# One cycle per batch from batch 2 on, with batch 2 loaded by transposed DMAs

## The chip, the cores and the metric

The kernel runs on one core of a Trainium2 chip. The metric is the time of one execution on the device in microseconds (us), the median of several runs. The core's engines work in parallel, each through its own list of instructions in order: PE (TensorE, matrix products; PEld are its weight loads), ACT (ScalarE), DVE (VectorE), POOL (GpSimd, here mostly an issuer of DMAs that convert types) and SP (SyncE, here an issuer of DMAs). They meet through semaphores.

## The reference

Attention with 12 heads over 8 batches of 448 tokens, with one added to the denominator, and behind it two dense layers with a squared ReLU between them:

```python
q, k, v: (8, 12, 448, 64) float32
scores = q @ k.T / 8
m = max(scores)
e = exp(scores - m)
attn = e / (sum(e) + exp(-m) + 1e-9)
x = (attn @ v) as (3584 tokens, 768)
h = x @ w_in                    # 768 -> 2048
out = (max(h, 0) ** 2) @ w_out  # 2048 -> 768, float32
```

The maximum cancels out: e / (sum + exp(-m)) is exp(s) / (sum exp(s) + 1), and the kernel computes it without m.

## The kernel before, in words

Work is in float16 with sums in float32. A **quad** is four heads of a batch (three quads a batch), a **chunk** is 64 keys (seven a quad). `QUADS` numbers the quads from batch 1 on: m = 0 to 2 are batch 1, and so on. The kernel gives Tile a schedule by hand: strings of steps, which are issued in exactly the order in which they stand. A step's letter names a function, its numbers are arguments:

- `s` scores of a chunk (PE, L400; 4 or 8 instructions on quarters of the array), `e` their exp (ACT, L432, one instruction of 128 x 896)
- `a` one of four adds that reduce a quad's seven exps (DVE, L435), `S` the sum over keys by a product with ones (PE, L451), `Z` Ln of sum + 1 and `M` exp of its negative, so the reciprocal (ACT, L460 and L465)
- `v` one chunk of exps times values (PE, L470), `X` values times reciprocal into `xt` (two DVE instructions, L482); `xt`'s six blocks of 128 rows come in pairs, a pair from each quad
- `j` two of the six products of a first-layer tile (128 of the 2048 columns, L513; a tile is `j n,0,2`, `j n,2,4`, `j n,4,6`, and each pair needs one quad's `X`), `k` ReLU (ACT or DVE, L521), `l` square into `gs` (DVE, L524)
- `o` some of the 16 products of an output tile (128 tokens by 384 columns, L554; each in four quarter-array instructions into two PSUM banks), `O` the first half of the result to SBUF (ACT if its last number is 1, otherwise DVE; L571), `Q` the second half added and the store issued on SP (L579)
- `T` and `U` transposes of a quad's q or k on PE and the copy to SBUF (L203, L210); `i`, `r`, `g` the first layer of half of batch 0 (L530, L500, L507); `p`, `b`, `y`, `z`, `n`, `x` the same attention steps for halves of batch 0 (L312 to L383)
- `d n` issues the n-th entry of `LOADS` (L626), or in a cycle one of `following` (L716)

**How q and k come in.** Batches in `ON_PE` (0, 1, 2) are loaded naturally by GpSimd in quads and transposed on PE. Later batches go through DRAM: `stage` (L144) copies q and k as float16 to a DRAM tensor (GpSimd), `transposed_load` (L163) reads three planes of it with a transposing DMA on SP, and `tail_keys` (L178) has GpSimd gather the last 64 keys of each head. `load_v_quads` brings v.

**Stages.** `ORDER` (L676) covers all of the attention of batches 0 to 3, the first layer of batches 0 and 1 and 14 output tiles. Then comes `CYCLE` (L750), run twice, for b = 4 and 6: first layer of batches b-2 and b-1 (32 tiles), attention of batches b and b+1, 14 output tiles. The tail (L793) is the first layer of batches 6 and 7 and the 15 output tiles that are left, plainly in a loop. In `ORDER` and in the tail a first-layer product takes all 128 columns of a tile (L496), in `CYCLE` two instructions of 64 columns (`cols`, L494). Tail output tiles use whole-array products (L567).

**Buffers that set who waits for whom.** PSUM: two score tiles (`sp`, also used by `S`), and from step `P0` on a ring of four banks: a `j` tile takes one (free after `k`), an `o` tile two (free after `O` and `Q`), a quad's `v` two (free after `X`). SBUF: two `rt` for ReLU, two `half` for the adds, two `rcp`, four output tiles `ot` (free when their store has landed), two `qk`, two `vn`. `gs` is a ring of two batches.

Of the kernel before, what the change touches and what calls it, by code (L numbers as in the profile page):

```python
# [16 lines left out]
def kernel(  # L17
# [654 lines left out]
    def other_ring():  # L672
# [8 lines left out]
        z2 b1,2 p6 s15 b1,3 p7 e15 y1 b3,0 n2 x2 b3,1 z1 s17 e17 b3,2 p12 p13 b3,3 n1 s18 p14 s16 e18 p15 x1 y3 T1,1,0 U1,1,0,0,7,0 e16 b4,0 z3 b4,1
        s19 e19 i0,6 n3 r0,6,0 s20 e20 s21 i0,7 s22 x3 b4,2 e21 p16 b4,3 e22 b5,0 r0,7,0 p17 p18 p19 d4 b5,1 g0,6 y4 z4 n4 s23 T1,1,1 e23 d13 s27 b5,2
        x4 i0,4 s28 p20 p21 g0,7 b5,3 e27 p22 p23 y5 U1,1,1,0,7,0 e28 z5 r0,4,0 n5 x5 s26 s29 e26 j20,0,2 j23,0,2 j23,2,4 j20,2,4 j20,4,6 e29 j23,4,6
        s25 k23,1 s24 g0,4 e25 e24 k20,0 P0 i1,7 j19,0,2 l23 a0,0 s32 e32 a0,1 s36 d6 j19,2,4 e36 j16,0,2 l20 j19,4,6 j17,0,2 s34 s33 k19,1 r1,7,0
        j17,2,4 j16,2,4 a0,2 l19 e34 j17,4,6 e33 j16,4,6 g1,7 s30 d11 k16,1 s31 e30 k17,0 T2,0,0 T1,2,0 T2,0,1 T1,2,1 l16 s35 e31 U2,0,0,0,7,0
        U1,2,0,0,7,0 s37 U2,0,1,0,7,1 e35 j18,0,2 j18,2,4 e37 j18,4,6 a0,3 i1,6 d19 S0 U1,2,1,0,7,0 v0,0 a1,0 v0,1 Z0 v0,2 l17 v0,3 v0,4 v0,5 k18,0 d7
        d12 v0,6 s40 s43 M0 r1,6,0 j27,0,2 a1,1 e43 j22,0,2 j22,2,4 j27,2,4 X0 e40 j27,4,6 l18 j22,4,6 g1,6 a1,2 s39 k27,1 s38 e39 a1,3 d20 T2,2,0 e38
        k22,0 T2,2,1 T2,1,1 T2,1,0 s41 U2,2,1,0,7,1 U2,2,0,0,7,0 s42 j26,0,2 l27 e41 j21,0,2 j26,2,4 j26,4,6 l22 S1 U2,1,0,0,7,0 e42 U2,1,1,0,7,0 Z1
        v1,0 v1,1 v1,2 v1,3 v1,4 d23 v1,5 k26,1 v1,6 a2,0 a2,1 a2,2 s44 s47 M1 l26 e44 j21,2,4 d22 j21,4,6 i1,4 X1 a2,3 k21,1 v2,0 v2,1 v2,2 r1,4,0 S2
        e47 v2,3 Z2 v2,4 v2,5 l21 v2,6 M2 o0,0,4 s46 o0,4,8 d14 s50 e46 e50 o0,8,12 X2 o0,12,16 s51 g1,4 s48 O0,1 Q0 j15,0,2 j0,0,2 j15,2,4 j4,0,2  # L690
        j15,4,6 j4,2,4 j4,4,6 j0,2,4 e51 e48 j0,4,6 s45 k15,1 l15 o2,0,4 s49 e45 e49 o2,4,8 s52 d21 o2,8,12 a3,0 e52 o2,12,16 k4,1 k0,0 s53 a3,1 s55
        d24 j10,0,2 O2,1 j1,0,2 Q2 j10,2,4 j1,2,4 j10,4,6 l0 j14,0,2 l4 j1,4,6 j11,0,2 e55 k10,0 j14,2,4 a3,2 j11,2,4 k1,1 j8,0,2 l10 j14,4,6 j11,4,6
        k11,1 j9,0,2 a3,3 j8,2,4 j9,2,4 e53 l1 j8,4,6 j9,4,6 k14,0 s57 l14 e57 l11 S3 Z3 v3,0 d25 v3,1 v3,2 v3,3 k9,0 k8,0 v3,4 v3,5 v3,6 M3 o1,0,4
        s54 o1,4,8 X3 s56 o1,8,12 o1,12,16 e54 a4,0 O1,0 s63 e56 o5,0,4 s58 o5,4,8 Q1 e63 a4,1 a4,2 s65 e58 a4,3 o5,8,12 e65 s60 o5,12,16 e60 O5,1 s59
        v4,0 v4,1 Q5 v4,2 v4,3 l9 S4 v4,4 e59 Z4 M4 v4,5 v4,6 o4,0,4 o4,4,8 s61 o4,8,12 o4,12,16 e61 s64 O4,1 X4 s62 j2,0,2 l8 Q4 j2,2,4 j2,4,6 j7,0,2
        k2,1 j5,0,2 e62 j7,2,4 j7,4,6 k7,0 l7 d27 j12,0,2 j6,0,2 e64 a5,0 j12,2,4 j5,2,4 l2 j5,4,6 k5,1 j6,2,4 j6,4,6 j12,4,6 a5,1 j13,0,2 j13,2,4
        j13,4,6 l5 a5,2 j3,0,2 j3,2,4 j3,4,6 k12,0 a5,3 s69 l12 k6,1 o3,0,4 l6 k13,1 k3,1 l3 S5 l13 o3,4,8 o3,8,12 o3,12,16 O3,0 Q3 e69 s70 Z5 s71 d26
        M5 v5,0 v5,1 v5,2 v5,3 e70 e71 v5,4 v5,5 v5,6 o9,0,2 o9,2,4 X5 o9,4,6 o9,6,8 s66 o9,8,10 s68 o9,10,12 o9,12,14 o9,14,16 e66 O9,0 o6,0,2 e68
        s67 s72 o6,2,4 o6,4,6 o6,6,8 e67 o6,8,10 Q9 a6,0 a6,1 e72 a6,2 s73 o8,0,2 o6,10,12 o6,12,14 o8,2,4 o6,14,16 s75 e73 O6,0 o8,4,6 o8,6,8 e75 s78
        Q6 o8,8,10 o8,10,12 a6,3 e78 o8,12,14 s79 o8,14,16 s77 v6,0 v6,1 v6,2 v6,3 e79 e77 v6,4 S6 v6,5 v6,6 Z6 M6 s74 O8,0 Q8 o7,0,2 o7,2,4 e74 X6  # L700
        o7,4,6 s76 e76 a7,0 o7,6,8 o7,8,10 o7,10,12 o7,12,14 a7,1 o7,14,16 s82 d28 o10,0,2 O7,1 o10,2,4 o10,4,6 Q7 o10,6,8 s80 a7,2 e82 o10,8,10
        o10,10,12 o10,12,14 o10,14,16 e80 s85 s83 o11,0,2 o11,2,4 e85 o11,4,6 o11,6,8 d31 O10,1 Q10 e83 s81 a7,3 d29 o11,8,10 o11,10,12 o11,12,14 e81
        o11,14,16 O11,1 Q11 s84 o12,0,2 s86 o12,2,4 o12,4,6 e84 e86 o12,6,8 o12,8,10 a8,0 o12,10,12 o12,12,14 o12,14,16 S7 a8,1 O12,0 o13,0,4 o13,4,8
        d30 o13,8,12 Z7 Q12 a8,2 o13,12,16 v7,0 v7,1 v7,2 v7,3 O13,1 v7,4 a8,3 v7,5 v7,6 M7 S8 Q13 v8,0 v8,1 Z8 v8,2 v8,3 M8 v8,4 v8,5 X7 v8,6 X8
# [7 lines left out]
    def period(b):  # L712
        m = NQ * (b - 1)
        first = EARLY + 2 * KC * (b - FIRST_PERIOD) // 2

        def following(n):  # L716
            ahead, what = ((1, n) if n < 6 else (2, 6) if n < 7 else (1, 6) if n < 8 else (2, n - 8))
            t = b + ahead
            if t < B and (n != 7 or b > FIRST_PERIOD):
                if what < 3:  # L720
                    transposed_load(t, what)
                elif what < 5:
                    tail_keys(t, (what - 2,))
                elif what == 5:
                    load_v_quads(t)
# [100 lines left out]
```

## Time and profile before

| | us |
|---|---|
| runs: median (lowest to highest of 3) | 392.35 (391.83 to 393.56) |
| the profiled execution, by the same clock as the runs | 393.06 |
| its span, first to last instruction | 391.3 |
| opening, to the first first-layer product of the first cycle | 0 to 135.7 |
| first cycle (b = 4): first layer / attention and output tiles | 135.7 to 172.1 / to 225.8 |
| second cycle (b = 6): first layer / attention and output tiles | 225.8 to 262.2 / to 315.5 |
| tail | 315.5 to 391.3 |

The page cuts the span into 40 slices of 9.8 us; a digit is the busy share in tenths (9 is 90% or more):

```profile
PE   9789999999999999999999999999999999999997
DVE  2887995765666766556968757566778788880000
ACT  5999998586689511349988731248988730001221
DMA  8999999999939899903129596941112200001132
```

ACT is full in the opening and in the attention parts of the cycles and nearly idle in their first-layer parts. The DMA engines are full for the first 100 us, in which all the weights and the first batches come in.

### The profile page before, as it was taken

What the parts mean: (1) busy time and instruction counts of PE and PEld (TensorE: products, weight loads), DVE (VectorE), ACT (ScalarE), POOL (GpSimd) and SP (SyncE); (2) the same over time, 40 slices, a digit from 0 to 9 for tenths busy, and PEclk for the clock granted to TensorE, in tenths of its full rate; (3) what the DMA queues carried; (4) which work ended last, traced back from release to release, by engine and by line L of the source; (5) the groups of instructions that cost most, each with busy time, mean ns of one, the idle gap of its engine ahead of it and who ended that gap; (6) DMA issues with size and microseconds to landing.
All of it is one profiled execution on the core that took longest, in us unless ns stands there. A gap on an engine that the chain in (4) does not pass through costs nothing.

```text
span 391.3 us, 14259 instructions
## 1 busy us (share of the span) xinstructions
PE 383.2 (98%) x6432; PEld 253.7 (65%) x6432; DVE 251.9 (64%) x468; ACT 228.5 (58%) x308; POOL 62.2 (16%) x96
## 2 busy tenths in 40 slices
PE   9789999999999999999999999999999999999997
PEld 5566656565789755667777665667777755556665
DVE  2887995765666766556968757566778788880000
ACT  5999998586689511349988731248988730001221
POOL 8544420025000701300001240310000000000000
PEclk9999999999999999999999999999999999999999
DMA  8999999999939899903129596941112200001132
GB/s 143 203 205 205 202 203 205 182 182 175 215 75 175 158 195 149 160 2 66 44 54 194 145 182 131 151 46 44 52 55 64 64 23 2 0 0 61 62 82 80
DMA packets 75052, 45.34 MB, mean 116 GB/s; under 512 B 47472, under 2 KB 72944, under 8 KB 74992
## 3 DMA queue, kind: packets, MB, share of 16 engines
q0 software_dynamic: 24752, 22.62, 37.4%
q1 hardware_dynamic: 49952, 21.59, 28.1%
q8 instruction: 50, 0.82, 0.9%
q10 hardware_dynamic: 288, 0.23, 0.2%
q14 instruction: 10, 0.08, 0.1%
HBM read 45.69 MB, written 17.93 MB: 163 GB/s over the span
## 4 chain that ended last, share of the span: by engine, by line
PE 86%; ACT 6%; DMA 2%; SPq 2%; DVE 1%; issue 1%; POOL 1%; ACTq 0%; POOLq 0%; DVEq 0%
PE mp L93 77%; PE sp L93 8%; ACT et L254 4%; SPq L166 2%; DMA nn<-in_k_dram 2%; PE mp L207 1%; DMA out_dram<-ot 1%; ACT rcp L372 1%; ACT nn L254 0%; DVE qk L217 0%; ACT rcp L365 0%; ACT ot L575 0%; DVE half L341 0%; ACT rcp L463 0%; DVE half L447 0%
## 5 line engine op out<-in xcount | busy, mean ns | idle before, releaser
L93 PE MATMUL mp<-wout,gs 64*64 64x384 f16 (+2 forms) x2928 | 165.2, 322 | 0.0
L93 PE MATMUL mp<-xt,win 128*64 128x448 f16 (+2 forms) x1188 | 148.3, 347 | 0.1
L93 PEld LDWEIGHTS <-gs 64*64 64x64 f16 (+1 forms) x2928 | 103.1, 106 | 34.5
L93 PEld LDWEIGHTS <-win 128*64 128x64 f16 (+1 forms) x1188 | 83.2, 106 | 63.5 <-issue 4.2
L254 ACT ACTIVATE et<-sp 128x896 f16<-128x896 f32 (+2 forms) x131 | 110.6, 889 | 12.3 <-PE sp L93 11.7
L505 DVE TENSOR_SCALAR rt<-mp 128x448 f16<-128x448 f32 x87 | 54.1, 622 | 17.4 <-PE mp L93 14.5
L509 DVE TENSOR_TENSOR gs<-rt 128x448 f16<-128x448 f16 x128 | 47.8, 390 | 22.1 <-ACT rt L503 20.2
L503 ACT ACTIVATE rt<-mp 128x448 f16<-128x448 f32 x41 | 21.8, 543 | 65.0 <-PE mp L93 55.7
L575 ACT ACTIVATE ot<-mp 128x384 f32<-128x384 f32 (+2 forms) x31 | 14.9, 480 | 71.6 <-PE mp L93 68.8
L93 PE MATMUL sp<-qk 64*64 64x224 f16 (+1 forms) x1056 | 53.7, 274 | 2.1 <-DVE qk L217 0.5
L93 PEld LDWEIGHTS <-qk 64*64 64x64 f16 x1056 | 32.7, 115 | 15.2 <-issue 6.5
L188 POOL COPY flatq<-qk 64x384 f16<-64x384 f16 x20 | 14.8, 739 | 172.7 <-DMA qk<-stage_k 126.0
L254 ACT ACTIVATE nn<-sp 128x896 f16<-128x896 f32 x42 | 37.1, 916 | 4.3 <-PE sp L93 4.2
L487 DVE TENSOR_TENSOR xt<-mp,rcp 128x448 f16<-128x448 f32 x42 | 24.2, 619 | 15.7 <-ACT rcp L466 10.3
L581 DVE SCALAR_TENSOR_TENSOR ot<-mp,ot 128x384 f32<-128x384 f32 x42 | 23.4, 556 | 15.3 <-ACT ot L575 12.4
...
L93 PE MATMUL mp<-et,vn 64*64 64x448 f16 (+1 forms) x448 | 24.5, 343 | 0.0
L577 DVE TENSOR_SCALAR ot<-mp 128x384 f32<-128x384 f32 x26 | 14.4, 555 | 14.3 <-PE mp L93 14.2
L463 ACT ACTIVATE rcp<-sp,one_b 128x896 f32<-128x896 f32 x21 | 21.1, 1007 | 2.8 <-PE sp L93 2.7
L466 ACT ACTIVATE rcp<-rcp 128x896 f32<-128x896 f32 x21 | 19.9, 949 | 0.5
L441 DVE TENSOR_TENSOR half<-et 128x1792 f16<-128x1792 f16 x15 | 16.3, 1088 | 4.3 <-ACT et L254 4.2
L443 DVE TENSOR_TENSOR half<-half,et 128x1792 f16<-128x1792 f16 x15 | 16.3, 1086 | 0.3
...
## 6 DMA issues: line engine op xcount, KB each, us to landing
...
```

The source lines that it names most:

```text
L93: return nc.tensor.matmul(out_, lhsT, rhs, start=start, stop=stop)
L254: nc.scalar.activation(out=out_, in_=in_, func=AF.Exp, scale=scale)
L441: nc.vector.tensor_add(esq[m], a[:, 0:w], a[:, w:2 * w])
L443: nc.vector.tensor_add(esq[m], esq[m], z[:, 0:w])
L463: nc.scalar.activation(out=rcp, in_=zp[:, :, 0:S], func=AF.Ln, bias=one_b)
L466: nc.scalar.activation(out=zqs[m], in_=zqs[m], func=AF.Exp, scale=-1.0)
L487: nc.vector.tensor_mul(xts[b][:, 2 * g + i, :], xqs[m][i][:, 0:S], zqs[m][:, i, :])
L503: nc.scalar.activation(out=rt[:, 0:m], in_=hp[:, 0:m], func=AF.Relu)
L505: nc.vector.tensor_scalar(out=rt[:, 0:m], in0=hp[:, 0:m], scalar1=0.0, scalar2=None, op0=ALU.max)
L509: nc.vector.tensor_mul(gs[:, f0:f0 + per, t0 % RING:t0 % RING + n], r, r)
L575: nc.scalar.activation(out=ot, in_=op[:, 0:w], func=AF.Copy, scale=OUT_SCALE)
L581: nc.vector.scalar_tensor_tensor(out=ot, in0=lo[:, 0:w], scalar=OUT_SCALE, in1=ot, op0=ALU.mult, op1=ALU.add)
```

## The change

`ON_PE` shrinks to batches 0 and 1. The opening now has all the attention of batches 0 and 1, the first layer of batch 0, and 6 output tiles. From batch 2 on there is one cycle per batch, run six times: first layer of batch b-1 in 64-column form (16 tiles), then attention of batch b with seven output tiles; loads are for batch b+1. The tail keeps the first layer of batch 7 and 9 output tiles (seven full, two narrow). The orders of the steps are new throughout.

```diff
-    ON_PE = (0, 1, 2)
+    ON_PE = (0, 1)
...
-    EARLY = 14
-    FIRST_PERIOD = 4
+    EARLY = 6
+    FIRST_CYCLE = 2
...
-    LOADS = ([lambda b=b, g=g: load_quad(b, g) for b in range(3) for g in range(NQ) if b + g]
+    LOADS = ([lambda b=b, g=g: load_quad(b, g) for b in range(2) for g in range(NQ) if b + g]
              + [lambda b=b, g=g: load_v_quads(b, g, g + 1) for b in range(2) for g in range(NQ)]
-             + [lambda: load_v_quads(2)]
              + [lambda i=i: load_win(i, NW) for i in range(NW)]
              + [lambda n0=n0, y=y: load_wout(n0, y, 2) for n0 in (0, HALF) for y in range(2)]
-             + [lambda: stage(3), lambda: transposed_loads(3), lambda: tail_keys(3), lambda: load_v_quads(3),
-                lambda: stage(4), lambda: transposed_loads(4), lambda: tail_keys(4), lambda: load_v_quads(4), lambda: stage(5)])
+             + [lambda: stage(2), lambda: load_v_quads(2)]
+             + [lambda i=i: transposed_load(2, i) for i in range(3)]
+             + [lambda i=i: tail_keys(2, (i,)) for i in (1, 2)])
...
     ORDER = """
...
+        n3 b4,1 r0,7,0 x3 s20 b4,2 e20 s21 i0,6 e21 b4,3 s22 p16 p17 d12 e22 p18 d11 p19 b5,0 y4 i0,4 r0,6,0 b5,1 z4 s23 n4 T1,1,1 e23 s27 b5,2 e27 x4
+        g0,7 b5,3 p20 d15 r0,4,0 p21 U1,1,1,0,7,0 p22 p23 g0,4 d4 y5 s29 z5 s28 g0,6 j7,0,2 n5 j7,2,4 j6,0,2 j6,2,4 x5 e28 j6,4,6 e29 j7,4,6 k6,0 l6
+        k7,1 P0 s25 s24 j10,0,2 j10,2,4 j10,4,6 d16 j0,0,2 j0,2,4 k10,0 d17 l7 j0,4,6 k0,0 l0 j11,0,2 j5,0,2 j11,2,4 l10 j5,2,4 j11,4,6 d8 k11,1
+        j3,0,2 j2,0,2 j5,4,6 j2,2,4 l11 e24 k5,1 j3,2,4 j4,0,2 j3,4,6 j1,0,2 e25 j4,2,4 j4,4,6 j2,4,6 k2,1 l5 k3,0 j1,2,4 l2 d18 d9 l3 k4,1 j1,4,6
+        k1,0 i1,6 l4 l1 i1,7 r1,7,1 T1,2,1 r1,6,0 T1,2,0 U1,2,0,0,7,0 s26 s30 e30 e26 a0,0 g1,7 o0,0,2 U1,2,1,0,7,1 o0,2,4 o0,4,6 o0,6,8 o0,8,10
+        o0,10,12 o0,12,14 g1,6 o0,14,16 a0,1 s37 s31 i1,4 O0,1 e37 r1,4,0 s32 g1,4 e31 o2,0,2 o2,2,4 s33 o2,4,6 a0,2 d19 o2,6,8 o2,8,10 e32 s34 e33 Q0
+        o2,10,12 d10 a0,3 o2,12,14 e34 o2,14,16 O2,0 Q2 s35 v0,0 v0,1 v0,2 e35 S0 v0,3 v0,4 v0,5 Z0 v0,6 M0 X0 s39 d22 o3,0,2 o3,2,4 s41 o3,4,6 e39
+        e41 o3,6,8 o3,8,10 o3,10,12 o1,0,2 o3,12,14 o3,14,16 s43 O3,0 Q3 e43 s36 o1,2,4 e36 o1,4,6 o1,6,8 o1,8,10 a1,0 o1,10,12 a1,1 o1,12,14 s42 a1,2
+        o1,14,16 O1,1 s38 a1,3 o5,0,2 Q1 e42 d23 o5,2,4 e38 o5,4,6 s40 e40 d25 o5,6,8 a2,0 S1 o5,8,10 o4,0,2 o5,10,12 o4,2,4 Z1 o5,12,14 o5,14,16 s44
+        d20 o4,4,6 o4,6,8 a2,1 M1 O5,1 o4,8,10 o4,10,12 o4,12,14 Q5 a2,2 v1,0 e44 a2,3 v1,1 o4,14,16 d24 O4,1 v1,2 v1,3 v1,4 v1,5 d21 Q4 S2 v2,0 v2,1
+        v2,2 v1,6 v2,3 Z2 v2,4 M2 v2,5 v2,6 X1 X2
     """
...
-    def period(b):
+    def cycle(b):
         m = NQ * (b - 1)
-        first = EARLY + 2 * KC * (b - FIRST_PERIOD) // 2
+        first = EARLY + KC * (b - FIRST_CYCLE)
...
         def following(n):
+            if b + 1 < B:
+                if n < 3:
+                    transposed_load(b + 1, n)
+                elif n < 5:
+                    tail_keys(b + 1, (n - 2,))
+                elif n == 5:
+                    load_v_quads(b + 1)
                 else:
-                    stage(t)
+                    stage(b + 1)
...
-            "j": lambda n, c0, c1: later_in(*block(n), c0, c1, True),
+            "j": lambda n, c0, c1: later_in(b - 1, n, c0, c1, True),
...
     CYCLE = """
+        j4,0,2 j4,2,4 j5,0,2 j5,2,4 j2,0,2 d5 j4,4,6 k4,1 j5,4,6 j2,2,4 l4 j6,0,2 j6,2,4 k5,0 j11,0,2 j6,4,6 j2,4,6 k2,0 l2 l5 k6,1 l6 j9,0,2 j9,2,4
...
+        k12,1 l13 j8,0,2 j8,2,4 d6 j10,2,4 d1 l12 k1,0 l1 j8,4,6 j10,4,6 k8,0 s0,5 o0,0,2 e0,5 s0,0 k10,0 l8 e0,0 o0,2,4 o0,4,6 o0,6,8 o1,0,2 s0,4
...
+        O6,1 s2,6 o4,8,10 e2,6 d3 o4,10,12 Q6 o4,12,14 d4 a2,2 o4,14,16 O4,1 a2,3 Q4 M1 v1,0 v1,1 v1,2 v1,3 v1,4 v1,5 S2 v1,6 v2,0 v2,1 v2,2 v2,3 v2,4
+        v2,5 X1 Z2 M2 v2,6 X2
     """
-    for b in range(FIRST_PERIOD, B, 2):
-        STEPS = period(b)
+    for b in range(FIRST_CYCLE, B):
+        STEPS = cycle(b)
...
-    for b in (B - 2, B - 1):
-        for f0 in range(NFFB):
-            tile_in(b, f0)
+    for f0 in range(NFFB):
+        tile_in(B - 1, f0)
```

In the new `LOADS` d0 to d4 are quads of batches 0 and 1, d5 to d10 their v, d11 to d14 quarters of `w_in`, d15 to d18 of `w_out`, d19 the stage of batch 2, d20 its v, d21 to d23 its three transposed loads (q, then the two planes of k), d24 and d25 its tail keys. In a cycle d0 to d2 are the transposed loads, d3 and d4 the tail keys, d5 v and d6 the stage of batch b+1.

More of the change, by code (lines that the diff above doesn't have):

```diff
@@ L525, in later_squared @@
         squared((b, "all", f0), S * b, S, f0, 1)
-    def of_tile(n):
-        return (1, n) if n < NFFB else (0, n - NFFB)
     def half_in(half, pair, c0, c1):
@@ L655 @@
         "y": lambda n: half_sum(n % NQ, n // NQ),
-        "j": lambda n, c0=0, c1=DCH: later_in(*of_tile(n), c0, c1),
-        "k": lambda n, act: later_relu(*of_tile(n), act),
-        "l": lambda n: later_squared(*of_tile(n)),
+        "j": lambda n, c0=0, c1=DCH: later_in(0, n, c0, c1),
+        "k": lambda n, act: later_relu(0, n, act),
+        "l": lambda n: later_squared(0, n),
         "d": lambda n: LOADS[n](),
@@ L681 @@
[L681 to L704, printed above, removed]
+        d0 W8 c0,0,1 d5 c1,0,1 c1,4,0 t0,0,0 t1,0,0 u0,0,0,0 t1,0,4 u1,0,0,0 c0,4,1 t0,0,4 u1,0,4,1 d1 s0 u0,0,4,1 t0,1,0 u0,1,0,0 t1,1,0 d2 e0 d7 s1
@@ new lines @@
+        u1,1,0,0 s2 t0,1,4 t1,1,4 e1 u1,1,4,1 u0,1,4,0 e2 s12 T0,1,0 T0,1,1 U0,1,0,0,4,0 U0,1,1,0,4,0 U0,1,1,4,7,0 s3 p0 b0,0 e12 s4 e3 p2 s6 p3 d6
+        U0,1,0,4,7,0 e4 s5 e6 b0,1 p1 b0,2 b0,3 e5 T0,2,0 y0 U0,2,0,0,4,0 T0,2,1 U0,2,1,0,4,0 U0,2,0,4,7,0 d14 U0,2,1,4,7,0 s9 z0 n0 b1,0 e9 x0 s11
+        T1,0,0 e11 s8 T1,0,1 e8 b1,1 s10 U1,0,1,0,7,0 e10 s13 b2,0 U1,0,0,0,7,0 b2,1 e13 b2,2 p8 s14 e14 b1,2 s7 p9 b2,3 e7 p4 s15 b1,3 p10 p11 y2 p5
+        p6 p7 y1 b3,0 e15 d3 z2 b3,1 s17 z1 s18 n2 x2 n1 b3,2 e17 p12 d13 p13 p14 p15 e18 s16 b3,3 e16 y3 x1 T1,1,0 s19 z3 U1,1,0,0,7,0 i0,7 e19 b4,0
@@ L708 @@
         STEPS[step[0]](*(int(y) for y in step[1:].split(",")))
-    def period(b):
+    def cycle(b):
         m = NQ * (b - 1)
-        first = EARLY + 2 * KC * (b - FIRST_PERIOD) // 2
+        first = EARLY + KC * (b - FIRST_CYCLE)
         def following(n):
[L717 to L725, printed above, removed]
-                else:
-                    stage(t)
-        def block(n):
-            return b - 2 + n // NFFB, n % NFFB
+            if b + 1 < B:
[5 more added lines that the diff above has]
+                    load_v_quads(b + 1)
+                else:
+                    stage(b + 1)
         return {
@@ L755 @@
-        l19 j18,0,2 j12,4,6 j18,2,4 j18,4,6 j9,0,2 k18,1 j9,2,4 j20,0,2 k12,1 l18 j20,2,4 j11,0,2 j9,4,6 l12 j20,4,6 d4 k9,0 j11,2,4 k20,1 l9 j5,0,2
-        j11,4,6 l20 k11,0 j29,0,2 j5,2,4 j5,4,6 k5,1 j29,2,4 l5 j29,4,6 l11 j1,0,2 j4,0,2 j1,2,4 k29,0 j25,0,2 j25,2,4 j1,4,6 j8,0,2 j4,2,4 j4,4,6
-        k1,1 j8,2,4 j2,0,2 j25,4,6 j2,2,4 l1 l29 j8,4,6 j2,4,6 k4,0 j28,0,2 k25,0 l25 l4 j28,2,4 j24,0,2 j28,4,6 e0,3 d5 k2,1 j24,2,4 k8,1 j23,0,2
-        j24,4,6 j10,0,2 j23,2,4 l8 j10,2,4 j10,4,6 l2 k24,0 j23,4,6 k10,1 s0,4 l24 k28,0 l10 k23,0 e0,4 s0,5 o0,0,2 o0,2,4 o0,4,6 o0,6,8 o0,8,10
@@ new lines @@
+        l11 k14,1 k0,0 l14 l0 j13,0,2 j1,0,2 j3,4,6 j1,2,4 j13,2,4 j15,4,6 j13,4,6 k15,1 k3,0 j12,0,2 j12,2,4 l15 j12,4,6 j10,0,2 j1,4,6 l3 k13,0
+        k12,1 l13 j8,0,2 j8,2,4 d6 j10,2,4 d1 l12 k1,0 l1 j8,4,6 j10,4,6 k8,0 s0,5 o0,0,2 e0,5 s0,0 k10,0 l8 e0,0 o0,2,4 o0,4,6 o0,6,8 o1,0,2 s0,4
+        o0,8,10 l10 s0,1 o0,10,12 o0,12,14 e0,4 e0,1 o0,14,16 s0,3 O0,1 Q0 o1,2,4 o1,4,6 e0,3 o1,6,8 s0,2 o1,8,10 o1,10,12 o2,0,2 o1,12,14 e0,2 s0,6
+        e0,6 o2,2,4 s1,6 o1,14,16 a0,0 o2,4,6 O1,0 o2,6,8 e1,6 s1,1 o2,8,10 o2,10,12 s1,2 e1,1 o2,12,14 o2,14,16 a0,1 s1,5 Q1 e1,2 o3,0,2 e1,5 O2,0
@@ new lines @@
+        o3,2,4 s1,4 e1,4 o3,4,6 a0,2 o3,6,8 o3,8,10 s1,3 a0,3 o3,10,12 o3,12,14 Q2 e1,3 s1,0 o3,14,16 O3,0 e1,0 Q3 v0,0 S0 v0,1 Z0 M0 v0,2 v0,3 v0,4
+        v0,5 v0,6 s2,0 e2,0 o5,0,2 d0 o5,2,4 o5,4,6 s2,4 o5,6,8 o5,8,10 e2,4 o5,10,12 s2,3 a1,0 X0 a1,1 a1,2 a1,3 d2 o5,12,14 o5,14,16 s2,1 e2,3
+        o6,0,2 o6,2,4 s2,2 e2,1 o6,4,6 O5,1 o6,6,8 o6,8,10 Q5 s2,5 o6,10,12 o6,12,14 o4,0,2 e2,2 S1 e2,5 o6,14,16 Z1 a2,0 a2,1 o4,2,4 o4,4,6 o4,6,8
+        O6,1 s2,6 o4,8,10 e2,6 d3 o4,10,12 Q6 o4,12,14 d4 a2,2 o4,14,16 O4,1 a2,3 Q4 M1 v1,0 v1,1 v1,2 v1,3 v1,4 v1,5 S2 v1,6 v2,0 v2,1 v2,2 v2,3 v2,4
```

31 lines of the change are left out of this document (5 added, 26 removed).

## The prediction

> **What bounds the kernel now.** First the engines' shares (busy us, share of the span, instructions), then the busy time of each engine by stage.
>
> ```profile
> PE 383.2 (98%) x6432; PEld 253.7 (65%) x6432; DVE 251.9 (64%) x468; ACT 228.5 (58%) x308; POOL 62.2 (16%) x96
> ```
>
> ```profile
> 0.00:33.40 33.40, 28.89 (x577) 20.05 (x578) 23.90 (x57) 28.80 (x46) 19.19 (x32) 1.00 1.14 187
> 33.40:135.70 102.30, 101.57 (x1829) 68.67 (x1826) 71.06 (x123) 81.18 (x106) 23.97 (x35) 1.00 1.06 179
> 135.70:172.10 36.40, 36.40 (x386) 21.65 (x384) 22.22 (x49) 8.35 (x16) 5.39 (x9) 1.00 1.06 143
> 172.10:225.80 53.70, 53.70 (x1428) 39.59 (x1426) 39.69 (x62) 47.10 (x57) 5.16 (x8) 1.00 0.43 94
> ...
> 315.50:391.30 75.80, 72.96 (x436) 41.59 (x432) 33.31 (x66) 7.86 (x16) 0.00 (x0) 1.00 0.12 37
> ```
>
> Columns: stretch and length, busy us of PE, PEld, DVE, ACT, POOL, granted clock, DMA share, GB/s. The reader is to see three things. TensorE (PE) has no idle time in a cycle, neither in its first-layer stretch (135.7 to 172.1) nor in attention with output tiles (172.1 to 225.8); the clock is 1.00 throughout. Only the first 33.4 us leave PE room (28.89 busy), and there ACT (28.80) sets the pace. And ACT is second everywhere, 47.10 of 53.70 in attention. So a microsecond of PE work is a microsecond of time, unless the new order makes PE wait.
>
> The chain of waits in order of time (start, length, what) has the prices of the PE work, and the one place where something else ruled late:
>
> ```profile
> 40.75 1.62 PE mp L93 x8
> 42.37 0.50 PE sp L93 x8
> 42.87 1.68 PE mp L207 x56
> ...
> 124.70 3.77 SPq L166
> 128.57 0.54 SPq L549
> 129.15 3.47 DMA out_dram<-ot
> 132.72 0.50 ACT ot L575
> ```
>
> 56 transposes took 1.68 us, 30 ns each. Eight full-height first-layer products took 1.62, while long groups show 0.189 each (192 in the 36.3 us of the tail), so entering such a group from 64-row work costs 0.1; two score chunks take 0.50 before a full-height group and 0.38 among 64-row work, so leaving costs 0.1 as well. The lines from 124.70 show SP: three transposed loads in a row (4.21, 2.80, 3.77 us) hold back stores, ACT waits for an output buffer, and PE then loses 0.3 and 0.4 us at 133.3 and 133.9.
>
> The same PE work in its forms (busy, mean ns of one | idle):
>
> ```profile
> L93 PE MATMUL mp<-xt,win 128*64 128x448 f16 x768 | 73.0, 353 | 0.0
> L93 PE MATMUL mp<-xt,win 128*128 128x448 f16 x348 | 67.9, 353 | 0.0
> ...
> L93 PEld LDWEIGHTS <-win 128*64 128x64 f16 x768 | 43.3, 110 | 29.1 <-issue 0.3
> ```
>
> Two 64-column products cost 0.190 together (384 in 36.44 us), one 128-column product 0.189 in the tail. The two forms are worth the same.
>
> **The change part by part**, against the profiled span of 391.3 us.
>
> 1. Batch 2 leaves the PE transposes. Three quads, two operands, 14 transposes: 84 x 30 ns = **2.5 us less**. Their six copies leave DVE and ACT (0.6 to 0.9 each), which were not the bound. Scores of batch 2 go from 4 instructions of 448 columns to 8 of 224; the PE timeline shows a chunk of either kind to the next start at 0.19. In their place come a stage, three transposed loads on SP, two tail copies and four loads of v on GpSimd instead of one, and its stores on SP go in rows of 224 instead of 64, fewer of them; costed at 0, covered under 8.
>
> 2. Changes of form. From 33.4 to 135.7 the PE timeline has 13 groups of full-height work between 64-row steps; in the new opening only three are left after the first first-layer tile (j7 and j6; j10 to T1,2; i1,4). 10 x 0.22 = **2.2 less**. The cycles had two such groups and the tail one; now six and one, four more at 0.19: **0.8 more**.
>
> 3. Waits of the old opening that go with their places: 0.2 at 36.4, 0.4 at 88.6 (DVE's last add of a sum) and the 0.7 at 133: **1.3 less**. The transposed loads of batch 2 stand apart in the new order (d22, d23, d21), and four output buffers cover one load's 3 to 4 us between two stores.
>
> 4. First layer of batches 1 and 6 goes from 128-column to 64-column form, 192 products at 0.001 more: 0.1 with rounding, **0.1 more**. Six output tiles go from the tail to the cycles: 2.60 in the tail, 16 x 0.1623 = 2.60 in quarters; nothing.
>
> 5. New cycles. One cycle: 16 tiles x 6 x 0.190 = 18.2, 42 score and value steps at 0.19 = 8.0, sums 0.6, seven tiles at 2.60 = 18.2, in all 45.0, half of the 90.1 that a pair takes now. What could break it is its edge: the next first layer needs the xt that the last step, X2, writes. The present end of the last cycle shows that path:
>
> ```profile
> 313.90 0.36 PE L93 MATMUL sp<-half,ones 64*64 64x448 f16 x4
> ...
> 314.32 1.01 ACT L463 ACTIVATE rcp<-sp,one_b 128x896 f32<-128x896 f32 x1 [0.19 <-PE sp L93]
> 315.36 0.95 ACT L466 ACTIVATE rcp<-rcp 128x896 f32<-128x896 f32 x1
> ...
> 316.34 1.16 DVE L487 TENSOR_TENSOR xt<-mp,rcp 128x448 f16<-128x448 f32 x2 [1.00 <-ACT rcp L466]
> ```
>
> From the start of the sum to the first half of xt: 316.96 - 313.90 = 3.06 us, to the second 3.60. In the new cycle PE has after S2: S2 itself, v1,6 and seven v2 (9 x 0.19 = 1.71), the change of form 0.1, then j4 and j5 up to the fourth product (8 x 0.19 = 1.52): 3.33. Then j2,0,2 needs the PSUM bank that X2's first half frees. Margin 0.27 less about 0.1 for the release: hidden, **0**, by only 0.15 to 0.2. At the tail the order is plain: four products (0.76) after 1.81, then a wait from 2.57 to 3.1, one product, and a wait to 3.65: **0.9 more**, once.
>
> 6. The new opening from its first output tile to its end is denser. PE: six tiles 15.6, 14 score chunks, 21 value steps and 3 sums 7.2, i1,4 1.25: 24.1 us. ACT: 16 exps at 0.84 (four in a row took 3.44, the last 0.92), three pairs Ln and exp at 1.9, four first halves at 0.38, one copy 0.9: 21.6. Walking the order down with these prices, PE comes early at o1,0,2, s40, S1 and v2,0, by 0.3 to 0.4 each. Example v2,0: after o4's end PE has four values and S2 (0.95), while O4 (0.2 + 0.38 + 0.1) and then Q4 (0.48 + 0.1 and 0.05) free its banks only at 1.3. With 0.4 at s28 and s25 **1.8 more**. Bounds: 0 (the stretch 50 to 60 has ACT at 9.60 of 10.00 without any PE wait) and 3.6, twice as much.
>
> 7. The first 33 us: same loads in the same sequence, same work; one 64x384 copy goes from DVE to ACT (0.48). Where ACT waits for scores anyway, 0; on ACT's path 0.5; better placed exps could win as much. I take **0.1 more**, bounds -0.7 and 0.7.
>
> 8. DMA order. GpSimd's loads land one after another at 200 KB/us (768 KB of wout in 3.9). After the last win quarter (36.3) come wout 40.2, quad 2 of batch 1 42.4, wout 46.3 and 50.2, v 51.3, wout 55.2, v 56.3, stage 62.9, v 64.0. The needs by PE's order: T1,2 at 48, o0 with its second half of wout at 50.5, v0,0 at 58, o3 at 60, v2,0 at 74. The tightest cover is 4 us, so 0; past it each microsecond late would be one of PE. In a cycle, d1 on SP waits for the stage (16 us from issue to landing at 223.7 to 239.4) with the stores of the following tiles behind it in SP's queue; it gets away at about 18 us, the first store is due at 22. If it were 5 us late, the fifth tile's buffer would still be free in time.
>
> Sum: -2.5 - 2.2 + 0.8 - 1.3 + 0.1 + 0.9 + 1.8 + 0.1 = **-2.3 us**: span 389.0. The profiled execution was 393.06 (1.8 around the span), the median of the runs 392.35; the same difference gives **390.1**.
>
> The Trainium skill, "TensorE: Matmul & The Clock Gate", section "Weight-path perf modes", says that fast weight load needs a weight of all 128 columns; 64-column halves would lose it. The trace shows loads of 110 ns for 64 columns and 98 for 128, and yet no idle time of PE; the sum by that rule would be rival B's, 395.9, by the rows 390.1.
>
> **Rivals.**
>
> A, slower: ACT late at the cycle's edge. It has four of seven first halves now, where a pair of batches had four of fourteen: 0.76 more a batch, so that of the 3.3 us a batch that it idled in attention (53.70 - 47.10, halved) 2.5 are left. If waits for scores keep it back by one exp and one first half at Z2 (0.84 + 0.38), X2 is 1.22 late, PE waits 1.22 - 0.16 = 1.06 in each of six cycles: +6.4, 396.5. It costs from 0.16 of lateness on and outweighs the gain and the bound of no change from 0.9. For it: the margin. Against: the walk has ACT idle before Z2, as at 314.32.
>
> B, slower: the 64-column form bound by weight loads, 2 x 110 = 220 ns against 190, on 192 more products: +5.8, 395.9. Against: those 768 already run at 0.095 each with idle 0.0.
>
> C, no change: the opening gives the gain back. Waits at 3.6 and start at +0.7: 2.4 more, 392.5. For it: ACT and PE nearly even there (21.6 to 24.1).
>
> D, faster by more: no waits in the opening, start 0.5 better: 387.7. For it: the stretch 50 to 60.
>
> **How the numbers follow.** Forecast 0.52 (its own range 388.9 to 391.5), C 0.22, A 0.16, B 0.03, D 0.07. A difference of 0.5% (1.96 us) is what a measurement tells from none. Below 390.4: three fifths of the forecast, and D, and a little more for edges that I priced at the upper side: 0.44. Above 394.3: A, B and a part of C: 0.21. Between: 0.35. The range 388.0 to 394.8 leaves out D's lower part and the costlier half of A and B.
>
> **What would show it.** Right: no PE wait over 0.15 us within cycles of 45.1 to 45.2, first layer of the first cycle at 75 to 76, tail of 42 to 43, 140 transposes on L207 instead of 224. Wrong: PE waiting for DVE's xt at each cycle's start (A), 64-column products above 0.095 (B), the first cycle after 77 (C), or PE waiting for a DMA.

## The result and the profile after

The changed kernel takes 393.74 us (median of 17 runs, 393.43 to 394.30); the kernel before, on the same chip in the same sequence, 392.45 (17 runs, 391.77 to 393.71). The ratio is 1.003, 95% interval 1.0021 to 1.0040: slower by 0.3%, which is inside the half per cent that the prediction called no change, and 3.6 us above its 390.1. The profiled execution took 393.68, with a span of 391.9.

First the engines' shares, then the busy time by stage, of the changed kernel (columns as before: stretch and length, busy us of PE, PEld, DVE, ACT, POOL, granted clock, DMA share, GB/s).

```profile
PE 382.0 (97%) x6912; PEld 258.0 (66%) x6912; DVE 246.6 (63%) x455; ACT 234.9 (60%) x321; POOL 61.6 (16%) x99
```

```profile
33.40:75.10 41.70, 41.11 (x682) 27.73 (x678) 26.70 (x48) 28.59 (x39) 3.54 (x5) 1.00 1.12 197
...
120.70:139.50 18.80, 18.54 (x200) 11.34 (x197) 10.65 (x25) 4.43 (x8) 3.74 (x6) 1.00 0.84 141
139.50:166.30 26.80, 26.80 (x713) 19.70 (x712) 18.93 (x30) 24.48 (x31) 2.46 (x4) 1.00 0.58 115
...
348.90:391.90 43.00, 39.50 (x244) 22.76 (x240) 17.44 (x35) 4.70 (x10) 0.00 (x0) 0.99 0.13 38
```

PE is still the bound: its busy time fell by 1.2 us, but its share fell too. In the attention of a cycle (139.5 to 166.3) it is full, 26.80 of 26.80. In the first layer of a cycle (120.7 to 139.5) it is not: 18.54 of 18.80, in a stretch where ACT works for 4.43 us and DVE for 10.65. The kernel before had 36.40 of 36.40 there. The clock is the full one, as before.

The chain of waits in order of time (start, length, what) names the place:

```profile
73.46 15.84 PE mp L93 x178
89.33 0.55 ACT rt L503
89.92 3.97 PE mp L93 x40
...
134.96 0.55 ACT rt L503
135.56 3.98 PE mp L93 x40
```

So the end of the kernel hangs on one relu of ACT (line 503) in each cycle, always with 40 products of the first layer still to come. The PE, ACT and DVE timelines around the first of these places (start, length, engine, line, what, in brackets the idle time before and its releaser):

```profile
75.09 14.57 PE L93 MATMUL mp<-xt,win 128*64 128x448 f16 x152
89.92 3.97 PE L93 MATMUL mp<-xt,win 128*64 128x448 f16 x40 [0.26 <-ACT rt L503]
```

```profile
89.33 0.54 ACT L503 ACTIVATE rt<-mp 128x448 f16<-128x448 f32 x1 [2.86 <-PE mp L93]
```

```profile
88.19 0.62 DVE L505 TENSOR_SCALAR rt<-mp 128x448 f16<-128x448 f32 x1 [1.00 <-PE mp L93]
```

152 products at the 0.0949 of the kernel before, from 75.09 on, would let the next start at 89.51; it starts at 89.92, a stall of 0.4 us. (The bracket shows 0.26, since it counts from a matmul's modelled end, and a matmul is shown with 0.35 us where one starts every 0.095. The 0.0949 itself still contains one change of form; experiment e1 below gives the stall as 0.45.) What PE waits for is k15, ACT's relu of tile 15, 89.33 to 89.87. DVE's relu of tile 3, k3, had been done since 88.81, so a PSUM bank was free more than half a microsecond before PE stopped, and still the product waited for the other one. The stall comes back in all six cycles, at 89.92, 135.56, 181.19, 226.83, 272.46 and 318.10, and a cycle takes (348.91 - 75.09) / 6 = 45.64 us.

The edge of a cycle, which the prediction feared, in the timeline of all engines:

```profile
118.93 0.36 PE L93 MATMUL sp<-half,ones 64*64 64x448 f16 x4
...
120.73 1.52 PE L93 MATMUL mp<-xt,win 128*64 128x448 f16 x14
...
121.36 1.16 DVE L487 TENSOR_TENSOR xt<-mp,rcp 128x448 f16<-128x448 f32 x2 [0.62 <-ACT rcp L466]
```

From the sum to the first half of xt: 121.36 + 0.62 - 118.93 = 3.05 us (3.06 was read from the kernel before), and PE passes from 120.73 on without a bracket. There is no stall.

The forms of the first layer (busy, mean ns of one | idle before, releaser), and the transposes:

```profile
L93 PE MATMUL mp<-xt,win 128*64 128x448 f16 x1152 | 111.3, 353 | 1.5 <-ACT rt L503 1.5
...
L207 PE MATMUL mp<-ident,nn 128*64 128x128 f16 x140 | 5.4, 222 | 0.0
```

140 transposes instead of 224, and 1.5 us of idle time before 64-column products where there was none: six times the 0.26 of the timeline.

### The profile page after: what moved, and what is told of

Read it like the earlier page. It is cut to its first block, busy times and chain, and to the rows that moved or that the text cites. A ratio compares the mean times of both kernels' runs of the same rounds, so it can differ in the third digit from the quotient of the medians.

```text
span 391.9 us, 15235 instructions
## 1 busy us (share of the span) xinstructions
PE 382.0 (97%) x6912; PEld 258.0 (66%) x6912; DVE 246.6 (63%) x455; ACT 234.9 (60%) x321; POOL 61.6 (16%) x99
## 4 chain that ended last, share of the span: by engine, by line
PE 91%; ACT 6%; DVE 1%; issue 0%; ACTq 0%
PE mp L93 79%; PE sp L93 9%; ACT et L254 3%; PE xp L93 2%; ACT rt L503 1%; PE mp L207 1%; ACT rcp L466 1%; DVE xt L487 1%; ACT rcp L463 0%; DVE qk L244 0%; ACT ot L572 0%; PE mp L234 0%; ACT rcp L368 0%; DVE xt L380 0%; ACT rcp L365 0%
## 5 line engine op out<-in xcount | busy, mean ns | idle before, releaser
L93 PE MATMUL mp<-wout,gs 64*64 64x384 f16 (+2 forms) x3216 | 171.0, 322 | 0.1
L93 PEld LDWEIGHTS <-win 128*64 128x64 f16 (+1 forms) x1380 | 89.5, 108 | 61.2 <-issue 7.5
L503 ACT ACTIVATE rt<-mp 128x448 f16<-128x448 f32 x48 | 26.1, 543 | 82.5 <-PE mp L93 56.7
L505 DVE TENSOR_SCALAR rt<-mp 128x448 f16<-128x448 f32 x80 | 49.2, 622 | 24.4 <-PE mp L93 22.9
L93 PE MATMUL sp<-qk 64*64 64x224 f16 (+1 forms) x1116 | 56.3, 266 | 2.4 <-ACT et L254 1.1
L93 PEld LDWEIGHTS <-qk 64*64 64x64 f16 x1116 | 35.0, 116 | 18.1 <-issue 7.0
L572 ACT ACTIVATE ot<-mp 128x384 f32<-128x384 f32 (+2 forms) x37 | 17.8, 480 | 40.0 <-PE mp L93 40.0
L578 DVE SCALAR_TENSOR_TENSOR ot<-mp,ot 128x384 f32<-128x384 f32 x48 | 26.7, 556 | 21.8 <-ACT ot L572 20.5
L93 PE MATMUL mp<-et,vn 64*64 64x448 f16 (+1 forms) x448 | 26.3, 344 | 0.0
L574 DVE TENSOR_SCALAR ot<-mp 128x384 f32<-128x384 f32 x20 | 11.2, 558 | 11.7 <-PE mp L93 11.5
```

The lines of the kernel that those rows point to most:

```text
L93: return nc.tensor.matmul(out_, lhsT, rhs, start=start, stop=stop)
L503: nc.scalar.activation(out=rt[:, 0:m], in_=hp[:, 0:m], func=AF.Relu)
L505: nc.vector.tensor_scalar(out=rt[:, 0:m], in0=hp[:, 0:m], scalar1=0.0, scalar2=None, op0=ALU.max)
L572: nc.scalar.activation(out=ot, in_=op[:, 0:w], func=AF.Copy, scale=OUT_SCALE)
L578: nc.vector.scalar_tensor_tensor(out=ot, in0=lo[:, 0:w], scalar=OUT_SCALE, in1=ot, op0=ALU.mult, op1=ALU.add)
```

## The experiments

Eight new kernels ran, and the kernel before twice more. None leaves out a part of the reference. "Cycle" below is the time from one cycle's first product to the next one's. The runs were taken in several sequences; the kernel before, run in each of them, had medians of 392.43 to 392.85, so that a difference between two medians of different sequences is uncertain by some tenths of a microsecond. Where that matters, the cycles of the profiles decide.

### e1_k3_first: the two relus ahead of the stall change places

```diff
-        ... j15,4,6 j13,4,6 k15,1 k3,0 j12,0,2 j12,2,4 ...
+        ... j15,4,6 j13,4,6 k3,0 k15,1 j12,0,2 j12,2,4 ...
```

> In every cycle PE waits 0.42 us before the twentieth product from the end of the first layer, which is j12,0,2, for the ReLU k15 on ACT. Here the steps k15 and k3 change places in the order, nothing else. Theory 1 (a new tile takes the PSUM bank that was freed first in the written order; j12 gets k15's bank, and k15 can start only when j15 ends, two products before j12): with k3 first j12 gets k3's bank, whose tile ended eight products earlier; the wait of 0.42 goes in all six cycles, a cycle is 45.2 us instead of 45.64, the time falls by 2.5 us to about 391.2. Theory 2 (a ring in turn: j12 had k3's bank anyway, and ACT is late for another reason): the wait stays within 0.1 us and so does the time, 393.7.

Measured: 391.10 us (8 runs, 390.89 to 391.86), ratio to the kernel before 0.9961 (0.9948 to 0.9975); 2.64 less than the changed kernel. PE's timeline of the same stretch:

```profile
76.01 18.35 PE L93 MATMUL mp<-xt,win 128*64 128x448 f16 x192
94.29 0.41 PE L93 MATMUL sp<-qk 64*64 64x224 f16 x8
...
121.20 18.35 PE L93 MATMUL mp<-xt,win 128*64 128x448 f16 x192
```

All 192 products stand in one group, the stall is gone in all six cycles, and a cycle takes 45.19. The two relus are on different engines, so neither starts earlier or later by being written first. DVE's and ACT's timelines show it:

```profile
89.11 0.62 DVE L505 TENSOR_SCALAR rt<-mp 128x448 f16<-128x448 f32 x1 [1.00 <-PE mp L93]
```

```profile
90.24 0.54 ACT L503 ACTIVATE rt<-mp 128x448 f16<-128x448 f32 x1 [2.86 <-PE mp L93]
```

Counted from the cycle's first product, k3 starts at 13.10 in both kernels, k15 at 14.24 in the changed kernel and at 14.23 here. What changes is which bank j12 gets: a new tile takes the bank that was freed first in the written order. In the changed kernel that is the bank of k15, which ACT can only read once tile 15's last product has ended, and only the four products of j13,4,6 (0.38 us) lie between that one and j12; here it is the bank of k3. The stall's size follows from the cycles: 45.64 - 45.19 = 0.45, six times 0.45 is 2.7.

This profiled execution began its first cycle 0.9 later than that of the changed kernel (76.01 against 75.09), with the same instructions up to there. Its PE timeline shows why, at the very start, where a load of k landed late (and one of v after it, 0.17 more):

```profile
10.77 0.58 PE L207 MATMUL mp<-ident,nn 128*64 128x128 f16 x14 [0.53 <-DMA nn<-in_k_dram]
```

Such differences between executions are why cycles and medians are compared below, rather than two spans.

### e2_k15_on_dve: tile 15's relu on the other engine

```diff
-        ... j15,4,6 j13,4,6 k15,1 k3,0 j12,0,2 ...
+        ... j15,4,6 j13,4,6 k15,0 k3,0 j12,0,2 ...
```

> The ReLU k15 moves from ACT to DVE, the order stays. Theory 1 (bank order): j12 still waits for k15's bank; a ReLU takes 0.62 on DVE and 0.54 on ACT, so the wait of 0.42 becomes about 0.5 in each cycle, now released by DVE, and the time goes up by 0.5 us or so to 394.2. Theory 2 (ACT is late): the wait goes, 391.2.

Measured: 394.16 us (one execution).

```profile
75.11 14.57 PE L93 MATMUL mp<-xt,win 128*64 128x448 f16 x152
90.02 3.97 PE L93 MATMUL mp<-xt,win 128*64 128x448 f16 x40 [0.34 <-DVE rt L505]
```

```profile
89.34 1.16 DVE L505 TENSOR_SCALAR rt<-mp 128x448 f16<-128x448 f32 x2 [2.14 <-PE mp L93]
```

The same stall at the same product, now with DVE as the releaser; DVE does k15 and k3 one after the other, and the product starts after the first of the two. It isn't that ACT is slow or late: whichever engine does k15, j12 stands behind it. That j12 keeps to the written order even where k3 is done first is shown by the changed kernel and e1, not by this run, in which k15 also ends first. From the cycle's start to the product that waited it is 90.02 - 75.11 = 14.91 us, 0.08 more than with ACT (89.92 - 75.09 = 14.83), as much as the relu is longer on DVE, 0.62 against 0.54.

### e3_full_columns: the first layer of the cycles in 128-column products

```diff
-            "j": lambda n, c0, c1: later_in(b - 1, n, c0, c1, True),
+            "j": lambda n, c0, c1: later_in(b - 1, n, c0, c1),
```

> The first layer in the cycles takes one product of 128 columns instead of two of 64. If both forms cost the same, as in the prediction (0.189 against 0.190), a cycle changes by less than 0.2 us, the time by less than 1.0: 393.7 plus or minus 1. If the 64-column form pays for its weight loads (220 against 190 ns for a product, on 96 products a cycle), this version wins 2.9 us a cycle, 17 in all, less 0 if only a part shows. The wait before j12 stays in any case.

Measured: 393.34 us (10 runs, 393.08 to 393.94), ratio to the kernel before 1.0021 (1.0008 to 1.0034); 0.4 less than the changed kernel. The forms:

```profile
L93 PE MATMUL mp<-xt,win 128*128 128x448 f16 x732 | 141.3, 352 | 2.2 <-ACT rt L503 1.5 <-DVE xt L487 0.6
```

The stall at k15 is the same, 1.5 us by the brackets, and a cycle takes 45.59 instead of 45.64. The 64-column form costs 0.05 us a cycle, 0.0005 for each of 96 pairs of products. Rival B wanted 30 ns for a pair.

### e4_tail_interleaved: e1, and other products where the tail waits

```diff
-    for f0 in range(NFFB):
+    for f0, c0 in ((0, 0), (0, 2), (1, 0), (1, 2), (2, 0), (0, 4), (1, 4), (2, 2), (2, 4)):
+        later_in(B - 1, f0, c0, c0 + 2)
+        if c0 == 4:
+            later_relu(B - 1, f0, False)
+            later_squared(B - 1, f0)
+    for f0 in range(3, NFFB):
         tile_in(B - 1, f0)
```

> On top of k3 before k15: the tail's first layer starts with four products of tile 0, four of tile 1 and two of tile 2 before the last two of tile 0, as the cycles do. In the tail PE waits 0.45 and 0.34 us for the two halves of xt; theory: ten products (1.9 us) instead of four before the first use of the last pair cover it, both waits go (0.8 us), 390.4. If banks or the ReLU of tile 0 hold it instead, some of the 0.8 comes back as a wait a few products later.

Measured: 390.21 us (6 runs, 390.06 to 390.45), ratio to the kernel before 0.9939 (0.9924 to 0.9953); 0.9 less than e1. The tail's start in PE's timeline, first of the changed kernel, then of this one:

```profile
348.91 0.93 PE L93 MATMUL mp<-xt,win 128*128 128x448 f16 x4
350.22 0.35 PE L93 MATMUL mp<-xt,win 128*128 128x448 f16 x1 [0.38 <-DVE xt L487]
350.75 2.43 PE L93 MATMUL mp<-xt,win 128*128 128x448 f16 x12 [0.18 <-DVE xt L487]
```

```profile
346.46 6.79 PE L93 MATMUL mp<-xt,win 128*128 128x448 f16 x35
```

The two waits for the halves of the last xt are gone, since products of other tiles, on rows that are there already, cover them. In the changed kernel they were 350.22 - 348.91 - 4 x 0.189 = 0.55 and 350.75 - 350.22 - 0.189 = 0.34, together the 0.9 that the prediction gave them and that the median lost here.

### e5_84_transposes_more: e4, and one quad's 28 transposes issued four times

```diff
-        for c in range(KC):
-            for j in range(2):
-                nc.tensor.transpose(...)
+        for _ in range(4 if (b, g) == (1, 2) else 1):
+            for c in range(KC):
+                for j in range(2):
+                    nc.tensor.transpose(...)
```

> On the version with k3 before k15 and the interleaved tail (390.2): the 28 transposes of the last quad of batch 1 are each issued four times, 84 more, the number that the change takes away with batch 2; the result is the same. If transposes stand on the path at 30 ns each, as the prediction's first term has it, the time rises by 2.5 us, to 392.7, all of it before the first cycle. If they fill time in which PE would have waited, it rises by less than 1.

Measured: 392.70 us (10 runs, 392.33 to 393.82), ratio to the kernel before 1.0002 (0.9992 to 1.0012). That is 2.49 more than e4, against 84 x 30 ns = 2.5. In the profiles the group of 28 takes 0.91 to the next step (48.20 to 49.11), the group of 112 takes 3.25 (47.99 to 51.24): 2.34 for 84, 28 ns each, and the first cycle starts later by just that, counted from the transposes at 31 (31.39 to 75.34 against 31.18 to 77.48). So 84 transposes cost their PE time in the new opening, and nothing behind them takes it up. They stand at another place than those that the change removes, and without their copies, which this run does not price.

### e6_bare_edge: e4, with tile 4 finished before tile 5 begins at each cycle's start

```diff
-        j4,0,2 j4,2,4 j5,0,2 j5,2,4 j2,0,2 d5 j4,4,6 k4,1 j5,4,6 j2,2,4 ...
+        j4,0,2 j4,2,4 j4,4,6 k4,1 j5,0,2 j5,2,4 j2,0,2 d5 j5,4,6 j2,2,4 ...
```

> On the same version: each cycle begins with six products of one tile instead of four and four of two tiles and two of a third before the last pair. If the path from the sum of the last quad to xt is 3.06 and 3.60 us long, as the prediction reckons, PE has 1.81 + 0.76 = 2.57 us of work ahead and waits 0.5 and 0.35 us at each of six edges: 5 us more, 395.2. If that path is shorter than reckoned (the margin of 0.15 us too small), the waits are shorter by as much.

Measured: 395.20 us (4 runs, 395.13 to 396.52), ratio to the kernel before 1.0067 (1.0047 to 1.0086); 5.0 more than e4.

```profile
120.90 0.95 PE L93 MATMUL mp<-xt,win 128*64 128x448 f16 x8
122.21 0.38 PE L93 MATMUL mp<-xt,win 128*64 128x448 f16 x2 [0.36 <-DVE xt L487]
122.74 1.51 PE L93 MATMUL mp<-xt,win 128*64 128x448 f16 x14
```

Now the edge shows. Eight products at 0.0945 (192 of them and one change of form in the 18.28 us of e1's group) would let the next start at 121.66; it starts at 122.21, a stall of 0.55, and after two more products there is one of 122.74 - 122.21 - 0.19 = 0.34. Together 0.89, and a cycle grows from 45.19 to 46.08, by just that. The first cycle loses 0.5 (one wait, for the second half of xt), so 5 x 0.89 + 0.5 = 4.95 of the 5.0. In the changed kernel the eight products of tile 5, 0.76 us, stand before the first one that needs X2's first half (j2,0,2, by its bank): it is hidden with 0.76 - 0.55 = 0.21 to spare.

### e7_opening_moved: e4, with three places of the opening moved

```diff
-        ... o3,8,10 o3,10,12 o1,0,2 o3,12,14 o3,14,16 s43 O3,0 Q3 e43 s36 o1,2,4 ...
+        ... o3,8,10 o3,10,12 o3,12,14 o3,14,16 s43 O3,0 Q3 e43 o1,0,2 s36 o1,2,4 ...
-        ... o5,4,6 s40 e40 d25 o5,6,8 a2,0 S1 o5,8,10 o4,0,2 o5,10,12 o4,2,4 ...
+        ... o5,4,6 o5,6,8 s40 e40 d25 a2,0 o5,8,10 o5,10,12 S1 o4,0,2 o4,2,4 ...
-        ... Q4 S2 v2,0 v2,1 v2,2 v1,6 v2,3 ...
+        ... Q4 S2 v1,6 v2,0 v2,1 v2,2 v2,3 ...
```

> On the same version, three moves in the opening at its four known waits: o1,0,2 behind the end of o3 (its bank is freed by X0), s40 and S1 two and four products of o5 later (they wait for ACT's exps), v1,6 ahead of v2,0 (which waits for Q4). Theory: the waits of 0.26, 0.35, 0.26 and 0.21 us are places where PE comes a little early, and other work covers them: 0.8 to 1.0 us less, 389.3. Rival: ACT's exps set the end of the opening there, and the waits come back at S1, S2 or the first values: less than 0.4 us gained.

Measured: 389.29 us (4 runs, 389.11 to 389.63), ratio to the kernel before 0.9909 (0.9892 to 0.9925). That is 0.92 less than e4 (1.2 by the two ratios), and the first cycle starts at 74.36 instead of 75.34. Of the four waits that this was meant to remove, 0.04 is left at s40 and 0.11 and 0.17 at value steps. This is the fastest version: faster than the kernel before by 0.9% (0.75 to 1.08%) and than the changed kernel by 4.45 us.

### before_again and before_third_look: the kernel before, unchanged

> The kernel before, profiled once more. The prediction took a difference against a profiled execution of 393.06 us and put it on a median of 392.35. If executions of this kernel differ by where the opening's loads land, this profile differs from the first one before 135.7 us alone, with cycles of 90.1 and a tail of 75.8 as before; a profile near 391.8 would show the opening up to 1.3 us shorter. Otherwise the difference is spread over the cycles.

> The kernel before, a third profile. The second one was 0.5 us shorter than the first in the opening, most of it where ACT and DVE wait for an output buffer at 133 us (one wait of PE, 0.3, instead of two, 0.3 and 0.4). If that wait is what moves the executions of before, this one has one, two or no such waits, and a time that goes with them within 0.3 us; the cycles stay at 90.1.

Measured: 392.61 and 393.14 us (one execution each; the profile that the prediction worked from took 393.06). One line each of ACT's timeline, of the profile that the prediction used, then of before_again and of before_third_look:

```profile
132.72 0.49 ACT L575 ACTIVATE ot<-mp 128x384 f32<-128x384 f32 x1 [2.66 <-DMA out_dram<-ot]
```

```profile
132.26 0.49 ACT L575 ACTIVATE ot<-mp 128x384 f32<-128x384 f32 x1 [2.25 <-DMA out_dram<-ot]
```

```profile
132.79 0.49 ACT L575 ACTIVATE ot<-mp 128x384 f32<-128x384 f32 x1 [2.85 <-DMA out_dram<-ot]
```

The wait for an output buffer behind SP's transposed loads is 2.25, 2.66 or 2.85 us long, and the executions took 392.61, 393.06 and 393.14. What PE loses by it, in PE's timeline of before_again:

```profile
132.68 0.39 PE L93 MATMUL sp<-half,ones 64*64 64x448 f16 x4
132.87 2.04 PE L93 MATMUL mp<-nn,vn 64*64 64x448 f16 x28
134.56 0.73 PE L93 MATMUL sp<-qk 64*64 64x224 f16 x16
135.22 0.95 PE L93 MATMUL mp<-xt,win 128*64 128x448 f16 x8
```

The sum of a quad and its seven value steps, at 0.19 each, need 1.52 us. From the sum to the scores 1.88 us pass here (132.68 to 134.56), so PE loses 0.4; in the profile that the prediction used it is 2.30 (132.72 to 135.02), 0.8 lost, in before_third_look 2.49 (132.60 to 135.09), 1.0 lost. The first cycle starts at 135.22, 135.68 and 135.75, and from there on the three profiles are alike (90.1 to the second cycle). So the wait of 0.7 us that the prediction took out of the old opening is 0.4 to 1.0, by execution. The changed kernel has no such place, and its 17 runs lie within 0.9 us where those of the kernel before spread over 1.9.

### e8_scores_in_first_layer: e4, with two score chunks moved into the first layer

```diff
-        j11,2,4 j9,4,6 j11,4,6 k9,0 k11,1 j7,0,2 l9 ...
+        j11,2,4 j9,4,6 j11,4,6 k9,0 k11,1 s0,5 j7,0,2 l9 ...
-        ... k0,0 l14 l0 j13,0,2 j1,0,2 ...
+        ... k0,0 l14 l0 s0,0 j13,0,2 j1,0,2 ...
-        ... j10,4,6 k8,0 s0,5 o0,0,2 e0,5 s0,0 k10,0 l8 e0,0 ...
+        ... j10,4,6 k8,0 o0,0,2 e0,5 k10,0 l8 e0,0 ...
```

> On the version with k3 before k15 and the interleaved tail (390.2): in each cycle the first two score chunks, s0,5 and s0,0, move into the first layer, to two separate places, their exps stay behind it. That makes two groups of full-height products more in each cycle, four changes of form. If a change of form costs 0.095 us, as the prediction's second term has it, a cycle gets 0.38 longer and the time 2.3, to 392.5. If changes of form cost nothing and the gaps in the opening before had another cause, the time stays at 390.2 or falls a little, since the exps' scores are ready earlier.

Measured: 393.35 us (10 runs, 392.68 to 393.62), ratio to the kernel before 1.0023 (1.0009 to 1.0037); 3.1 more than e4 (3.3 by the two ratios, 3.0 by the six cycles). PE's timeline of the first cycle:

```profile
75.81 5.84 PE L93 MATMUL mp<-xt,win 128*64 128x448 f16 x60
81.58 0.40 PE L93 MATMUL sp<-qk 64*64 64x224 f16 x8
81.92 5.11 PE L93 MATMUL mp<-xt,win 128*64 128x448 f16 x52
```

(The view begins inside the first layer.) No stall stands in a bracket, yet a cycle takes 45.69 (74.65 to 120.34) instead of 45.19. A chunk of scores that takes 0.19 among other 64-row work takes 81.92 - 81.58 = 0.34 here, and 60 products from 75.81 on end at 81.48 by their pace, 0.1 before the chunk starts. Four changes of form more in each of six cycles, 24 in all, cost 3.1 us: 0.13 each, not the 0.1 read from the old chain.

## Why the prediction missed, step by step

**The step that failed is the fifth, the new cycles.** It summed the products ("in all 45.0") and said "What could break it is its edge". The inside of the first layer was taken as products that follow each other, with each new tile finding a free bank. There the change wrote a product behind a relu whose input PE finishes only 0.38 us earlier, and the bank that this relu frees is the one that the product gets: 0.45 us in each of six cycles. Measured were 45.64 a cycle where the prediction had 45.1 to 45.2, 2.9 us in all; e1 takes out the stall by exchanging two words and gives 45.19 and 2.64 us, and e2 shows that it is not ACT's doing. That was no rival either, though it could have been read from the new order of steps: a walk over the relus that asks, for each new tile, which bank comes free first in the written order, and when.

**The rest of the miss is the step from span to median.** The forecast was a span of 389.0; with the 1.8 around it, 390.8. It was lowered to 390.1 because the profiled execution of before lay 0.7 over its median. But the three profiles of the kernel before differ, by 0.5 us, in when their first cycle starts after the output-buffer wait at 133, and the sum had already taken that wait out at its size in the profiled execution. An execution of the kernel before in which this wait is short has less of it to lose; the changed kernel has none, and its profiled execution is 0.06 from its median. So a part of this 0.7 was taken off twice. How large that part is isn't shown: runs that were not profiled are as short as 391.77, and the shortest of the three profiles, 392.61, would without its 0.4 still take 392.2, so something else moves the executions of the kernel before as well. The cycles' 2.9 and this 0.7 are the 3.6 that was missed. The spans add up. The prediction did not write out how its 389.0 divides, but by its parts a cycle is 45.15 (half of 90.1 and half of a group's 0.19), the tail 75.8 - 18.1 - 15.6 + 0.9 = 43.0, and 75.1 is left for the opening: 75.1 + 6 x 45.15 + 43.0 = 389.0. What came is 75.1 + 6 x 45.64 + 43.0 = 391.9.

**Transposes (1).** Right in their price: e5 gives 2.3 (profiles) to 2.5 (medians) for 84, issued at another place.

**Changes of form (2).** Right in sign, small in size: at the 0.13 of e8, ten groups fewer are 2.6 instead of 2.2 and four more 1.0 instead of 0.8, a net 0.2 more gain. This doesn't show in the opening, which met 75.1; but executions with this same opening (the changed kernel, e1 to e4, e6, e8) begin their first cycle at 74.65 to 76.01, so meeting it to the tenth is luck, and the old opening's groups weren't undone one by one.

**Old waits (3).** The 0.7 at 133 is 0.4 to 1.0, as above. The others weren't tried by themselves.

**64-column form (4).** Right: e3. The sentence on the Trainium skill ("TensorE: Matmul & The Clock Gate", section "Weight-path perf modes") stood beside rival B, with the sum by its rule. A price like B's is not there in this kernel: 0.0005 us a pair.

**The edge and the tail (5).** Right in both. The edge costs nothing, rival A did not come, and e6 shows that the cover is needed: without it 0.89 a cycle is lost, and the margin comes out at 0.21, where the prediction had 0.15 to 0.2. The tail's 0.9 came and e4 gets it back.

**The new opening (6).** Right in its places; its 1.8 was not measured by itself. The chain of the changed kernel shows what was walked down by hand:

```profile
59.04 0.96 ACT rcp L466
60.03 1.17 DVE xt L487 x2
61.23 1.17 PE mp L93 x23
...
65.77 1.62 ACT et L254 x2
67.44 0.38 PE sp L93 x4
...
72.34 0.49 ACT ot L572
72.85 0.57 DVE ot L578
73.46 15.84 PE mp L93 x178
```

At 61.23 o1,0,2 waits for DVE's xt, at 67.44 S1 stands behind two exps, and at 73.46 v2,0 behind the last output quarter, as the prediction's example had it; with s40 (66.62) these are 0.26, 0.26, 0.21 and 0.35, together 1.1 of the 1.8. Waits of 0.2 at s28 (33.06) and of 0.2 ahead of j10 (36.45, behind a relu of ACT), where the prediction had 0.4 at s28 and s25, make it 1.5; where the rest lies isn't shown. e7 takes 0.92 of them away, so rival D's waitless opening was not far off, but had to be written first.

**The first 33 us and the DMA order (7, 8).** No product of a cycle or of the new opening waits for a DMA in the changed kernel's profile, and the loads land as walked down: wout at 39.7, 45.9, 49.7 and 54.7, the stage at 62.9, each within 0.5 us of the list. What moves is the first 11 us, by up to 0.9 between executions (e1's late loads).

**Chances.** Of the signs that were named, the first layer of the first cycle at 75 to 76, a tail of 42 to 43 and 140 transposes came; cycles of 45.1 to 45.2 without a wait of PE didn't. The result lies between 390.4 and 394.3, which had a chance of 0.35. Rival C gave a time nearer to the result, 392.5, but by a mechanism that did not happen: the opening kept its gain, and the cycles gave it back.
